# Attention and two mixtures on one core: the two layers of neighbouring blocks alternate, the gate's products follow the norm, and tasks that free a bank go first

## The chip, the cores and the metric

The kernel runs on one core of a Trainium2 chip. The metric is the device time of one execution in microseconds (us). Before the change it was 953.02 us, the median of three runs (952.83 to 954.03).

## The reference, cut to what matters

```
for each chunk c of 32 tokens:                 # attention, 4 x 8 heads, 768 tokens, head size 64
    k_full = mem_k (8 tokens) + k[16 left .. 8 right of the chunk]
    a   = softmax(q_c @ k_full.T / sqrt(64));  out = a @ v_full
x = out as (3072 tokens, 512)
h = x @ w_in                                   # first mixture: 512 -> 2048
g = where(h >= 1, h, where(h <= -1, 0, (h + 1)**2 / 4))
x = g @ w_out                                  # 2048 -> 512
xn = x / (norm(x) + 1e-6); logits = xn @ en.T / tau   # gate over 8 experts
e  = argmax(logits); gate = softmax(logits)[e]
out = gate * (relu(x @ w1[e]) @ w2[e])         # second mixture: 512 -> 1024 -> 512
```

All results are float32. The kernel splits a float32 operand into a high and a low float16 part and adds the products high*high, high*low and low*high.

## The kernel before, in words

**Blocks.** The 3072 tokens are cut into 8 blocks (`j`, 0 to 7) of 384 tokens. A block is 4 attention units (`u`) of 96 tokens, each of two halves (`a`, 4 heads each), and 3 tiles of 128 tokens for the second layer and the gate. The 2048 hidden features are 16 chunks (`fc`) of 128.

**Stages of a block.** First layer: for each chunk two steps of six matmuls (`l1_mm`, L441), into one PSUM bank of 128x384. Its evacuation is `l1_ev` (ScalarE), `l1_mx` (VectorE, L453, reads the bank last), `l1_mn` (VectorE, L457), `l1_hi` (ScalarE, L460) and `l1_lo` (VectorE, L463). Second layer: block 0 goes chunk by chunk, nine matmuls each over its three tiles at once (three banks); later blocks go tile by tile (`l2_mm`, L467 to L469). The second layer of block 0 also needs the weights `w_out`, which ScalarE and VectorE unpack from 64-bit floats (`conv_*`, L398 to L425), as they do `w_in` before.

**Gate of a block**, in this order: squares (`sq`, ScalarE), root on GpSimd (`grt`), norm on VectorE (`gno`, L504 to L519), transposes of the tiles by DMA (`xt`), the products with the experts on TensorE (`dot`, L495, 24 small matmuls into one bank), logits on VectorE (`glo`, L526 to L534, which read that bank), the first maximum (`gfi`, L542 to L547), weights (`gst`), ranks on TensorE (`grk`, L561 and L562, one more bank), and places on VectorE (`gpo`, L568 to L576, which read that bank).

**Banks.** PSUM is dealt in rings: `mm` with three banks (first layer, second layer, `dot`, `grk`), `PT` with two (attention's transposes, and two of five chunks of the first layer from block 2 on), `S` with two (scores), `X` with one. A ring is served in turn: the next task in `mm` takes the bank of the task three before it, and waits until what reads that one (its `frees`) is done.

**Attention** of a later block runs between the layers of a block. On VectorE a half costs `mx` (L290), `rc` (L312, L315) and four `ab` (L347); a unit costs copies and remainders of k, q and v (`k1` L248, `k` L253, `t1` L257, `t` L261, `vl` L266) and `xhl` (L385). On TensorE a half is a group of score matmuls (L281, or L283 and L284) and one of L367, or L369 to L371.

**Order.** `mixture` records all this as tasks with needs, engine and a cost from the table `COST`; `Plan.order` lists them twice backward and forward and writes one order for every engine. Among the tasks that could start at about the same time it takes the one that is wanted first. Every engine then works through its list in order, so a task that waits holds all that stand behind it on its engine. From the loop over the second mixture's later slots on, the order is written by hand.

Of the kernel before, what the change touches and what calls it, by code (L numbers as in the profile page):

```python
# [28 lines left out]
UB = 4  # L29
BT = UB * QU  # L30
NB = NT // BT
TB = BT // 128
NTILE = NT // 128
NFC = FF1 // 128
# [12 lines left out]
    cf=0.4, mk=1.5, k=2.2, K=4.0, c=2.3, v=1.1, pk=0.95, pt=0.73, pv=0.53, pk1=0.34, pkl=1.13, pt1=0.27, ptl=0.87, pvl=0.6,  # L47
    scc=1.72, scp=0.88, sc=0.47, mx=0.6, mb=0.1, sm=1.37, r1=0.1, rc=0.15, nm=0.6, trc=0.65, tr=0.34, ev=0.37, eh=1.0, el=0.8,
    td=1.25, avc=1.3, avp=0.68, av=0.52, xh=0.38, xl=0.47, ca=(0.58, 0.43), cv=0.34, cb=0.6, cs=0.6, cc=0.53, cd=0.6,
    l1=0.98, r4=0.47, mu=0.47, mn=0.47, hi=0.43, lo=0.47, l2=1.95, l2t=1.3, x2=0.49, sq=0.62, x2l=0.6, xt=1.25, dot=2.4,  # L50
    pad=0.4, emb=0.5, esq=0.6, ert=0.9, ein=1.9, etr=0.4, ehi=0.2, elo=0.2, grt=0.9, gno=1.6, glo=1.2, gfi=1.5, gst=0.8,
    grk=0.1, gpo=1.7, ga=2.6, w=2.3, wh=0.95, wl=1.13, xd=1.25, m1=2.62, mh=0.49, ml=0.6, m2=1.3, mo=0.57, ms=1.0, fbc=0.193,
    fbk=2.2, fbm=1.87, fbl=3.4, fbp=2.1, fbi=0.7, fbt=3.4, fac=0.175, fak=2.6, fal=1.4, fap=0.42, fai=0.5, fat=1.436)
# [1 line left out]
WIN = 0.019  # L55
PASSES = 3
CAE, ABUF = 'AD', 2
RINGS = dict(S=2, mm=3, PT=2)
PTJ = 2
BIG = 12582912.0  # L60

C_ID, C_I128, C_I39, C_I8, C_VT, C_TR = 0, 128, 256, 296, 304, 328
# [2 lines left out]


NUDGE = {}


class Plan:  # L70
# [14 lines left out]
    def run(self, pre, post, wanted, rings):  # L85
        free, held = defaultdict(float), defaultdict(list)
        missing = {t["n"]: len(t[pre]) for t in self.tasks}
        at = {}
        ready = [t for t in self.tasks if not missing[t["n"]]]
        done = []  # L90
        while ready:
            best = None
            for t in ready:
                if rings and t["ring"]:
                    h = held[t["ring"]]
                    k = len(h) - RINGS[t["ring"]]
                    extra = [self.named[x] for x in h[max(k, 0):max(k + len(t["frees"]), 0)] if x in self.named]
                    if any(x["n"] not in at for x in extra):
                        continue
                else:  # L100
                    extra = ()
                for w, c in list(zip(t["where"], t["cost"]))[:None if rings else 1]:
                    b = free[w]
                    for x in t[pre] + list(extra):
                        e, v = at[x["n"]]
                        d, u = (x, v) if rings else (t, w)
                        b = max(b, e + LAT[1 if u == "S" else 2 * (v == w)])
                    if best is None or (round(b / WIN), wanted[t["n"]], b + c) < best[0]:
                        best = ((round(b / WIN), wanted[t["n"]], b + c), t, b, c, w)
            _, t, b, c, w = best  # L110
            ready.remove(t)
            free[w] = b + c
            at[t["n"]] = (b + c, w)
            done.append((b, len(done), t, w))
            if rings and t["ring"]:
                held[t["ring"]] += t["frees"]
            for x in t[post]:
                missing[x["n"]] -= 1
                if not missing[x["n"]]:
                    ready.append(x)  # L120
        assert len(done) == len(self.tasks)
        return at, done
# [28 lines left out]
def moe_chain(ctx, tc, qd, kd, vd, win, wout, emb, tau, w1, w2, tmask, kmask, qp, kp, cf32, cf16, out):  # L151
# [275 lines left out]
    l1p = {}  # L427

    def l1_ring(j, fc):
        return "PT" if j >= PTJ and fc % 5 > 2 else "mm"  # L430

    def l1_mm(j, fc, part):
        xh, xl = xt[j]
# [224 lines left out]
    def mixture():  # L658
# [4 lines left out]
        def add(k, n, f, where, needs=(), cost=None, ring=None, frees=()):  # L663
            done[k, n] = pl.add((k, n), f, where, COST[cost or k], [x if isinstance(x, dict) else done.get(x) for x in needs], ring, frees)
# [107 lines left out]
        def weights(s, c, needs):  # L772
# [4 lines left out]
            add("wh", 8 * s + c, lambda w: split_w(s, c), "A", [("w", 8 * s + c), *needs])  # L777
            add("wl", 8 * s + c, lambda w: split_lo(s, c), "D", [("wh", 8 * s + c)])

        for u in range(UB):  # L780
            attention(u)
        for c in range(NRAW):
            load(c)
        for j in range(NB):
            i = start[j]
            if j == 0:
                for c in range(NFC):
                    conv(c)
            if j == NB - 1:
                n = (("fat", 0),)  # L790
            else:
                n = ()
            for fc in range(NFC):
                m = NFC * j + fc
                xs = [(x, u) for x in ("xh", "xl") for u in range(UB * j, UB * j + UB)]
                pe_slot(("l1", j, fc, 0), i, [("cc", fc), *xs, *n], "l1", ring=l1_ring(j, fc), frees=[("mu", m)])
                pe_slot(("l1", j, fc, 1), i + 1, [("cd", fc)], "l1")
                i += 2
                evac(j, m, fc)
                if j == NB - 1 and fc == 0:  # L800
                    for h in range(2):
                        add("ga", h, lambda w, h=h: gather(h), "G", [prev, ("ga", h - 1)])
                    for c in range(8):
                        add("w", c, lambda w, c=c: load_w(0, c), "S", [prev, ("w", c - 1)])
                if j == NB - 1 and fc % 2 == 1:
                    weights(0, fc // 2, [prev])
                    if fc == NFC - 1:
                        inputs(0, [prev])
            if j + 1 < NB:
                for u in range(UB * (j + 1), UB * (j + 2)):  # L810
                    attention(u)
            if j == 0:
                for c in range(NFC, 2 * NFC):
                    conv(c)
                for fc in range(NFC):
                    k = dict(ring="mm", frees=[("x2l", t) for t in range(TB)]) if fc == 0 else {}
                    pe_slot(("l2", 0, fc), i + fc, [("cd", NFC + fc), ("lo", fc), ("hi", fc)], "l2", **k)
                cds = [("cd", c) for c in range(2 * NFC)]
                add("pad", 0, lambda w: pads(), "G", cds)
                add("emb", 0, lambda w: emb_load(), "S", [("cf", 0)])  # L820
                add("esq", 0, lambda w: emb_sq(), "A", [("emb", 0)])
                add("ert", 0, lambda w: emb_root(), "G", [("esq", 0)])
                add("ein", 0, lambda w: emb_inv(), "D", [("ert", 0)])
                add("etr", 0, lambda w: emb_tr(), "P", [("ein", 0)], ring="mm", frees=[("elo", 0)])
                add("ehi", 0, lambda w: emb_hi(), "A", [("etr", 0)])
                add("elo", 0, lambda w: emb_lo(), "D", [("ehi", 0)])
            for t in range(TB):
                n = TB * j + t
                if j > 0:
                    for fc in range(0, NFC, 2):  # L830
                        m = NFC * j + fc
                        k = dict(ring="mm", frees=[("x2l", n)]) if fc == 0 else {}
                        pe_slot(("l2", j, t, fc), i, [("lo", m), ("lo", m + 1)], "l2t", **k)
                        i += 1
                last = ("l2", j, t, NFC - 2) if j else ("l2", 0, NFC - 1)
                add("x2", n, lambda w, n=n: l2_ev(n, p2[n % TB]), "A", [last, ("gst", j - 2), ("x2", n - 1), ("pad", 0)])
                add("sq", n, lambda w, n=n: g_sq(n, p2[n % TB]), "A", [("x2", n), ("sq", n - 1), ("glo", j - 2)])
                add("x2l", n, lambda w, n=n: l2_lo(n, p2[n % TB]), "D", [("x2", n), ("sq", n)])
                add("xt", n, lambda w, n=n: g_xt(n), "S", [("x2l", n), ("dot", j - 1), ("xt", n - 1)])
            add("dot", j, lambda w, j=j: g_dot(j), "P", [("xt", n), ("elo", 0)], ring="mm", frees=[("glo", j)])  # L840
            add("grt", j, lambda w, j=j: g_root(j), "G", [("sq", n)])
            add("gno", j, lambda w, j=j: g_norm(j), "D", [("grt", j), ("ein", 0)])
            add("glo", j, lambda w, j=j: g_logit(j), "D", [("gno", j), ("dot", j), ("gpo", j - 2), ("gst", j - 2)])
            add("gfi", j, lambda w, j=j: g_first(j), "D", [("glo", j), ("gfi", j - 1)])
            add("gst", j, lambda w, j=j: g_store(j), "D", [("gfi", j)])
            add("grk", j, lambda w, j=j: g_rank(j), "P", [("gfi", j), ("mk", 0)], ring="mm", frees=[("gpo", j)])
            add("gpo", j, lambda w, j=j: g_pos(j), "D", [("grk", j), ("gpo", j - 1)])
            if (j + 1) * TB == TA:
                add("fac", 0, lambda w: fa_count(), "P", [("gfi", j)], ring="S", frees=[("fak", 0)])
                add("fak", 0, lambda w: fa_key(), "D", [("fac", 0)])  # L850
                add("fal", 0, lambda w: fa_look(), "D", [("fak", 0), ("gpo", j)])
                add("fap", 0, lambda w: fa_place(), "D", [("fal", 0)])
                add("fai", 0, lambda w: fa_ids(), "P", [("fap", 0)], ring="S", frees=[("fat", 0)])
                add("fat", 0, lambda w: fa_table(), "D", [("fai", 0)])
# [492 lines left out]
```

## Time and profile before

| | |
|---|---|
| time, median of three runs | 953.02 us (952.83 to 954.03) |
| the profiled execution's own time | 952.98 us |
| its span, first to last instruction | 951.1 us |
| TensorE matmuls busy | 874.3 us (92%) |
| VectorE busy | 697.5 us (73%) |
| ScalarE busy | 557.5 us (59%) |
| mean granted TensorE clock | 0.983 |

The span is the time that the instructions take; the execution's own time is 1.9 us more. A clock of 1.00 is 2.4 GHz and 0.50 is 1.2 GHz. The busy shares are means over stages that differ, so stages are looked at one by one.

### The profile page before, as it was taken

To read this page: it belongs to the slowest core of one execution; us is meant where nothing else is said; L and a number is where in the kernel's file an instruction comes from. 1 tells how busy PE (TensorE), PEld (TensorE's weight loads), DVE (VectorE), ACT (ScalarE), POOL (GpSimd) and SP (SyncE) were. 2 spreads that over 40 slices of the span, in tenths; PEclk is the share of its full clock that TensorE was granted. 3 is DMA by queue.
4 is the path that set the end of the run, shared out by engine and by line. 5 is a ranking of instruction groups with operands and counts; after the bars stand their busy time and mean duration, and the time that the engine had idled before them with its cause. 6 is when DMAs were issued, how large, how long until landed. Compare 5 with 4: busy or idle time off the path is not lost.

```text
span 951.1 us, 17049 instructions
## 1 busy us (share of the span) xinstructions
PE 874.3 (92%) x6072; PEld 525.5 (55%) x6072; DVE 697.5 (73%) x1601; ACT 557.5 (59%) x1397; POOL 71.7 (8%) x70
## 2 busy tenths in 40 slices
PE   2899999997588999989999999999999899999995
PEld 2666555444354555555555454554666567766663
DVE  6999999988997896897895294494764745556650
ACT  4767869777857846846855142363434655555551
POOL 0000000000000000000000100200021222222221
PEclk9999999999799999999999999999999999999998
DMA  9964536357534723632411200466222223322550
GB/s 267 263 196 124 194 101 161 101 156 191 141 123 109 153 73 65 185 85 44 70 45 28 40 34 12 138 196 162 72 68 78 68 68 85 84 67 68 138 163 25
DMA packets 118700, 105.64 MB, mean 111 GB/s; under 512 B 92286, under 2 KB 92548, under 8 KB 118608
## 3 DMA queue, kind: packets, MB, share of 16 engines
q1 hardware_dynamic: 114608, 91.80, 36.7%
q0 software_dynamic: 4000, 12.69, 4.1%
q8 instruction: 49, 0.80, 0.4%
q14 instruction: 43, 0.35, 0.1%
HBM read 112.09 MB, written 12.94 MB: 131 GB/s over the span
## 4 chain that ended last, share of the span: by engine, by line
issue 77%; DVE 10%; DMA 6%; POOL 3%; PE 1%; ACT 1%; POOLq 0%; SPq 0%; DVEq 0%; ACTq 0%
DMA out<-o,fbid 5%; DVE cvt L409 2%; POOL xg L1118 2%; DVE cvt L413 1%; DMA out<-o,faid 1%; DVE wo L425 1%; DVE cvv L405 1%; DVE t L453 1%; DVE mx L290 1%; DVE r L457 1%; POOL nsa L499 1%; DVE wi L425 1%; DVE g L463 1%; PE S L281 1%; POOL out L1185 1%
## 5 line engine op out<-in xcount | busy, mean ns | idle before, releaser
L441 PEld LDWEIGHTS <-wi 128*128 128x128 f16 x1536 | 149.9, 99 | 110.5 <-issue 19.0
L441 PE MATMUL mm<-xhl,wi 128*128 128x384 f16 x1104 | 197.4, 335 | 8.2 <-DVE t L453 5.6
L467 PE MATMUL mm<-wo,g 128*128 128x512 f16 x384 | 146.4, 381 | 0.5 <-DVE t L453 0.5
L469 PE MATMUL mm<-wo,g 128*128 128x512 f16 x384 | 146.0, 380 | 0.0
L468 PE MATMUL mm<-wo,g 128*128 128x512 f16 x384 | 146.0, 380 | 0.0
L460 ACT ACTIVATE g<-r 128x384 f16<-128x384 f32 x128 | 66.9, 523 | 78.5 <-DVE r L457 78.4
L1158 DVE SCALAR_TENSOR_TENSOR g<-PT,g 128x512 f16<-128x512 f32 (+1 forms) x52 | 34.8, 670 | 93.0 <-ACT g L1153 93.0
L441 PE MATMUL PT<-xhl,wi 128*128 128x384 f16 x432 | 74.3, 326 | 0.0
L1110 DVE SCALAR_TENSOR_TENSOR wi<-stg,wi 128x1024 f16<-128x1024 f32 x56 | 66.1, 1219 | 8.2 <-ACT wi L1105 8.2
L463 DVE TENSOR_TENSOR g<-r,g 128x384 f16<-128x384 f32 x128 | 70.3, 549 | 1.9 <-ACT g L460 1.2
L457 DVE SCALAR_TENSOR_TENSOR r<-r,t 128x384 f32<-128x384 f32 x128 | 70.5, 551 | 0.7
L1153 ACT ACTIVATE g<-PT 128x512 f16<-128x512 f32 (+1 forms) x52 | 30.2, 581 | 68.5 <-PE PT L1147 68.5
L447 ACT ACTIVATE r<-mm,two 128x384 f32<-128x384 f32 x92 | 53.0, 577 | 26.4 <-PE mm L441 24.8
L342 ACT ACTIVATE ab<-e,rc 96x128 f16<-96x128 f32 x184 | 58.7, 395 | 13.1 <-issue 3.8
L306 ACT ACTIVATE e<-S,mx 96x128 f32<-96x128 f32 x184 | 64.1, 363 | 0.8 <-DVE ab L347 0.7
L469 PEld LDWEIGHTS <-g 128*128 128x128 f16 x384 | 37.6, 98 | 45.7 <-issue 0.6
L1110 DVE SCALAR_TENSOR_TENSOR wo<-stg,wo 128x1024 f16<-128x1024 f32 x48 | 56.4, 1219 | 8.4 <-ACT wo L1105 7.9
L467 PEld LDWEIGHTS <-g 128*128 128x128 f16 x384 | 37.5, 98 | 38.6 <-issue 0.3
L468 PEld LDWEIGHTS <-g 128*128 128x128 f16 x384 | 37.6, 98 | 36.3 <-issue 1.0
L1105 ACT ACTIVATE wi<-stg 128x1024 f16<-128x1024 f32 x56 | 57.0, 1046 | 0.0
L476 DVE SCALAR_TENSOR_TENSOR x2a<-mm,x2a 128x512 f16<-128x512 f32 x24 | 16.5, 687 | 55.0 <-ACT junk L484 54.9
L1182 ACT ACTIVATE o<-mm,xg 128x512 f32<-128x512 f32 x25 | 17.2, 687 | 66.2 <-issue 41.0
(263 smaller groups left out, 1786.2 us busy)
## 6 DMA issues: line engine op xcount, KB each, us to landing
stg<-w SPq DMA_DIRECT2D x104, 512.0 KB
kraw<-kd SPq DMA_DIRECT2D x23, 512.0 KB
qraw<-qd SPq DMA_DIRECT2D x23, 384.0 KB
vraw<-vd SPq DMA_DIRECT2D x30, 256.0 KB
x2d<-x2a SPq DMA_DIRECT2D x8, 780.0 KB
x2a<-win SPq DMA_DIRECT2D x8, 512.0 KB
x2a<-wout SPq DMA_DIRECT2D x7, 512.0 KB
kraw<-kp SPq DMA_DIRECT2D x7, 256.0 KB
```

The source lines that it names most:

```text
L306: act.activation(e[:QU, i, :], w["s"][:QU, i, :], AF.Exp, bias=nb[:QU, i:i + 1], scale=0.125 if plain(a // 2) else 1.0, accum_out=sm[:QU, ...
L342: act.activation(w["ab"][:QU, 0, i, :], w["e"][:QU, i, :], AF.Copy, scale=w["rc"][:QU, i:i + 1])
L441: pe.matmul(l1p[fc], w[fc][:, k, :], x[:, k, :], start=(part == 0 and n == 0), stop=(part == 1 and n == 5))
L447: act.activation(g32[fc], l1p[fc], AF.Relu, bias=two[:, 0:1], scale=2.0 ** -13)
L457: dve.scalar_tensor_tensor(out=r4, in0=r4, scalar=4.0, in1=t4s.pop(fc), op0=ALU.min, op1=ALU.mult)
L460: act.activation(gh[fc], g32[fc], AF.Copy)
L463: dve.tensor_tensor(gl[fc], g32.pop(fc), gh[fc], ALU.subtract)
L467: pe.matmul(p, gh[fc][:, ts], woh[fc], start=(fc == 0), stop=False)
L468: pe.matmul(p, gh[fc][:, ts], wol[fc], start=False, stop=False)
L469: pe.matmul(p, gl[fc][:, ts], woh[fc], start=False, stop=(fc == NFC - 1))
L1105: act.activation(hi, stg[c], AF.Copy, scale=64.0 if c < NK else 512.0)
L1110: dve.scalar_tensor_tensor(out=lo, in0=stg[c], scalar=sc, in1=hi, op0=ALU.mult, op1=ALU.subtract)
```

## The change

Four edits. (1) The first layer of block 1 is no longer behind the second layer of block 0 but between its chunks: after chunk `fc` of the second layer (from `fc` = 3 on) comes chunk `fc - 3` of block 1's first layer. Its banks come from the ring `PT` alone, since the second layer of block 0 holds all three banks of `mm`. The attention of block 2 is recorded after both. (2) `dot` needs `gno`, and its entry in the cost table is smaller. (3) Where the forward pass picks among tasks that could start together, `glo`, `gpo`, `x2l` and `elo`, which all free a bank of `mm`, come before all others. (4) The counting of steps (`start`) follows. No arithmetic is added or removed.

```diff
-    l1=0.98, r4=0.47, mu=0.47, mn=0.47, hi=0.43, lo=0.47, l2=1.95, l2t=1.3, x2=0.49, sq=0.62, x2l=0.6, xt=1.25, dot=2.4,
+    l1=0.98, r4=0.47, mu=0.47, mn=0.47, hi=0.43, lo=0.47, l2=1.95, l2t=1.3, x2=0.49, sq=0.62, x2l=0.6, xt=1.25, dot=0.65,
+AHEAD = 3
+RUSH = ("glo", "gpo", "x2l", "elo")
...
-                    if best is None or (round(b / WIN), wanted[t["n"]], b + c) < best[0]:
-                        best = ((round(b / WIN), wanted[t["n"]], b + c), t, b, c, w)
+                    r = (round(b / WIN), wanted[t["n"]] - 1e4 * (rings and t["key"][0] in RUSH), b + c)
+                    if best is None or r < best[0]:
+                        best = (r, t, b, c, w)
...
     def l1_ring(j, fc):
-        return "PT" if j >= PTJ and fc % 5 > 2 else "mm"
+        return "PT" if j == 1 or j >= PTJ and fc % 5 > 2 else "mm"
...
+        def first(j, fc, n=()):
+            i, m = start[j] + 2 * fc, NFC * j + fc
+            xs = [(x, u) for x in ("xh", "xl") for u in range(UB * j, UB * j + UB)]
+            pe_slot(("l1", j, fc, 0), i, [("cc", fc), *xs, *n], "l1", ring=l1_ring(j, fc), frees=[("mu", m)])
+            pe_slot(("l1", j, fc, 1), i + 1, [("cd", fc)], "l1")
+            evac(j, m, fc)
...
-            for fc in range(NFC):
-                m = NFC * j + fc
...
+            for fc in range(NFC if j != 1 else 0):
+                first(j, fc, n)
...
-            if j + 1 < NB:
+            if j + 1 < NB and j != 1:
                 for u in range(UB * (j + 1), UB * (j + 2)):
                     attention(u)
...
                     pe_slot(("l2", 0, fc), i + fc, [("cd", NFC + fc), ("lo", fc), ("hi", fc)], "l2", **k)
+
+                    if fc >= AHEAD:
+                        first(1, fc - AHEAD)
+                for fc in range(NFC - AHEAD, NFC):
+                    first(1, fc)
+                for u in range(2 * UB, 3 * UB):
+                    attention(u)
...
-            add("dot", j, lambda w, j=j: g_dot(j), "P", [("xt", n), ("elo", 0)], ring="mm", frees=[("glo", j)])
             add("grt", j, lambda w, j=j: g_root(j), "G", [("sq", n)])
             add("gno", j, lambda w, j=j: g_norm(j), "D", [("grt", j), ("ein", 0)])
+            add("dot", j, lambda w, j=j: g_dot(j), "P", [("xt", n), ("elo", 0), ("gno", j)], ring="mm", frees=[("glo", j)])
```

What this makes of the engines' lists is seen at three places. The line numbers of the changed kernel are 3 higher there. First TensorE at the second layer of block 0: `wo_94` and `wo_95` are the high and low weights of the second layer, `wi_86` low weights of the first, `PT<-cf,e` a transpose of attention. Before, between its chunks 3 and 4:

```order
L467 LDWEIGHTS g
L467 MATMUL mm<-wo_94,g 128x512
L468 LDWEIGHTS g
L468 MATMUL mm<-wo_95,g 128x512
L469 LDWEIGHTS g
L469 MATMUL mm<-wo_94,g 128x512
L325 MATMUL PT<-cf,e 128x96 x4
L467 LDWEIGHTS g
```

and now the end of block 1's first chunk, which stands between the same two chunks:

```order
L444 LDWEIGHTS wi_86
L444 MATMUL PT<-xhl,wi_86 128x384
L470 LDWEIGHTS g
L470 MATMUL mm<-wo_94,g 128x512
L471 LDWEIGHTS g
L471 MATMUL mm<-wo_95,g 128x512
L472 LDWEIGHTS g
L472 MATMUL mm<-wo_94,g 128x512
```

The twelve matmuls of a first-layer chunk moved in between; attention's transposes that stood there are ahead of it or behind. Second VectorE in the first layer of block 2, where the gates of blocks 0 and 1 stand. Before, the logits of block 1 (`lg`) and the places of block 0 (`rk`) came behind attention (`ab`, `mx`, `k`, `vl`):

```order
L290 TENSOR_REDUCE mx<-S 96x4
L253 SCALAR_TENSOR_TENSOR k_3095<-kraw,k_3095 64x1024
L347 SCALAR_TENSOR_TENSOR ab<-e,rc,ab 96x128 x4
L266 SCALAR_TENSOR_TENSOR vl<-vraw,vh 128x512
L526 COPY lg<-mm 128x24
L527 TENSOR_TENSOR lg<-lg,mm 128x24
L528 TENSOR_TENSOR lg<-lg,nrm 128x24
L530 TENSOR_REDUCE mxl<-lg 128x3
L533 TENSOR_TENSOR eq<-lg,mxl 128x24
L534 TENSOR_TENSOR lg<-lg,mxl 128x24
L568 TENSOR_TENSOR rk<-mm,oh 128x24
```

and now the places of block 0 come behind the first evacuation (`t`, `r`) of block 2's first layer:

```order
L479 SCALAR_TENSOR_TENSOR x2a<-mm,x2a 128x512
L456 SCALAR_TENSOR_TENSOR t_2766<-mm,r_2748 128x384
L293 TENSOR_REDUCE mx<-S 96x4
L460 SCALAR_TENSOR_TENSOR r_2748<-r_2748,t_2766 128x384
L350 SCALAR_TENSOR_TENSOR ab<-e,rc,ab 96x128 x4
L571 TENSOR_TENSOR rk<-mm,oh 128x24
L573 TENSOR_REDUCE pos<-rk 128x3
```

They moved from behind the evacuation of the fifth chunk to behind that of the first. The `dot` of block 1 and its logits left this layer: they now stand in the second layer of block 2. Third TensorE in the first layer of block 6, at the ranks of block 5 (`oh`, `rs`; `wi_80` and `wi_88` are the weights of chunks 4 and 5). Before they stood ahead of chunk 5, whose banks are of `mm` again:

```order
L441 LDWEIGHTS wi_88
L441 MATMUL PT<-xhl,wi_88 128x384
L561 LDWEIGHTS ch
L561 MATMUL mm<-oh,ch 128x24
L562 LDWEIGHTS ch
L562 MATMUL mm<-rs,ch 128x24
L441 LDWEIGHTS wi_80
L441 MATMUL mm<-xhl,wi_80 128x384
```

and now between the two steps of chunk 5:

```order
L444 LDWEIGHTS wi_80
L444 MATMUL mm<-xhl,wi_80 128x384
L564 LDWEIGHTS ch
L564 MATMUL mm<-oh,ch 128x24
L565 LDWEIGHTS ch
L565 MATMUL mm<-rs,ch 128x24
L444 LDWEIGHTS wi_80
L444 MATMUL mm<-xhl,wi_80 128x384
```

They moved back by one step of six matmuls, and past the point where chunk 5 takes its bank: so chunk 7 now takes the bank that chunk 5 held, and chunk 10 that of the ranks.

## Rows read from the trace of the kernel before

**Rows 1.** Part 1 of the page: busy us, share of the span, instructions.

```profile
PE 874.3 (92%) x6072; PEld 525.5 (55%) x6072; DVE 697.5 (73%) x1601; ACT 557.5 (59%) x1397; POOL 71.7 (8%) x70
```

**Rows 2.** Windows between first evacuations: engines' busy us (count), granted clock, DMA share, GB/s.

```profile
0.00:60.97 60.97, 38.12 (x203) 30.20 (x204) 49.54 (x114) 36.98 (x122) 0.32 (x6) 1.00 0.85 249
60.97:143.45 82.48, 79.41 (x533) 47.56 (x531) 82.33 (x179) 63.09 (x175) 2.80 (x3) 1.00 0.48 147
143.45:181.92 38.47, 35.34 (x276) 20.93 (x274) 38.33 (x97) 35.17 (x102) 0.00 (x0) 1.00 0.48 119
181.92:227.40 45.48, 40.76 (x319) 21.70 (x319) 40.05 (x113) 31.69 (x107) 1.29 (x1) 0.96 0.69 184
227.40:286.07 58.67, 43.59 (x341) 26.89 (x340) 56.31 (x160) 42.56 (x132) 0.00 (x0) 0.88 0.46 132
286.07:328.09 42.02, 39.77 (x307) 20.67 (x307) 32.09 (x80) 33.78 (x120) 0.79 (x1) 0.96 0.59 142
328.09:362.37 34.28, 31.55 (x204) 18.50 (x202) 30.61 (x85) 17.18 (x36) 0.06 (x1) 0.95 0.25 59
362.37:403.94 41.57, 41.35 (x322) 21.52 (x321) 32.06 (x79) 33.72 (x120) 0.78 (x1) 1.00 0.58 143
```

**Rows 3.** Timeline of TensorE: start, us, line, tiles, count, idle before and its releaser.

```profile
222.56 0.24 PE L369 MATMUL X<-at,vh 128*64 128x96 f16 x2 [3.52 <-DMA at<-ab]
...
233.62 0.75 PE L495 MATMUL mm<-ent,x2x 128*128 128x16 f16 x24
...
252.12 0.30 PE L369 MATMUL X<-at,vh 128*64 128x96 f16 x2 [4.22 <-DMA at<-ab]
```

**Rows 4.** Timeline of VectorE around 252 us.

```profile
252.75 0.17 DVE L526 COPY lg<-mm 128x24 f32<-128x24 f32 x1
...
253.91 0.17 DVE L568 TENSOR_TENSOR rk<-mm,oh 128x24 f32<-128x24 f32 x1
```

**Rows 5.** Windows of 5 us in the same stretch, columns as in group 2.

```profile
245.00:250.00 5.00, 1.71 (x20) 1.58 (x20) 4.97 (x16) 5.00 (x21) 0.00 (x0) 0.50 0.43 165
250.00:255.00 5.00, 2.88 (x25) 2.10 (x25) 4.62 (x18) 2.83 (x10) 0.00 (x0) 0.50 0.74 221
```

**Rows 6.** Groups of VectorE: busy us, mean ns of one, idle before.

```profile
L347 DVE SCALAR_TENSOR_TENSOR ab<-e,rc,ab 96x128 f16<-96x128 f32 x184 | 52.5, 342 | 3.3 <-ACT ab L342 3.2
...
L290 DVE TENSOR_REDUCE mx<-S 96x4 f32<-96x512 f32 x60 | 40.7, 678 | 15.8 <-PE S L281 9.0 <-PE S L284 6.7
...
L253 DVE SCALAR_TENSOR_TENSOR k<-kraw,k 64x1024 f16<-64x1024 f32 x23 | 28.1, 1223 | 0.7
...
L261 DVE TENSOR_TENSOR t<-qraw,t 64x768 f16<-64x768 f32 x23 | 21.7, 944 | 0.1
...
L266 DVE SCALAR_TENSOR_TENSOR vl<-vraw,vh 128x512 f16<-128x512 f32 x23 | 15.7, 681 | 0.8 <-ACT vh L243 0.7
```

**Rows 7.** Timeline of TensorE: a group of scores and the first layer behind it.

```profile
142.40 0.22 PE L283 MATMUL S<-k,t 67*96 67x128 f16 x1
...
142.87 1.14 PE L441 MATMUL mm<-xhl,wi 128*128 128x384 f16 x6
```

**Rows 8.** Timeline of TensorE: waits at the gates of later blocks.

```profile
342.27 3.77 PE L441 MATMUL mm<-xhl,wi 128*128 128x384 f16 x12 [1.95 <-DVE t L453]
...
418.12 2.11 PE L441 MATMUL mm<-xhl,wi 128*128 128x384 f16 x12 [1.95 <-DVE t L453]
...
553.05 0.17 PE L561 MATMUL mm<-oh,ch 128*128 128x24 f16 x1 [1.23 <-DVE oh L545]
...
620.52 0.17 PE L561 MATMUL mm<-oh,ch 128*128 128x24 f16 x1 [0.96 <-DVE oh L545]
...
623.28 2.11 PE L441 MATMUL mm<-xhl,wi 128*128 128x384 f16 x12 [0.22 <-DVE rk L568]
```

**Rows 9.** Timelines around the gate of block 5: the norm's end on VectorE, the products on TensorE.

```profile
546.43 0.23 DVE L519 TENSOR_SCALAR nrm<-nrm,rtau 128x3 f32<-128x3 f32 x1
...
547.17 0.74 PE L495 MATMUL mm<-ent,x2x 128*128 128x16 f16 x24 [0.20 <-DVE t L453]
```

More of the change, by code (lines that the diff above doesn't have):

```diff
@@ L784, in mixture @@
         for j in range(NB):
-            i = start[j]
+            i = start[j] + 2 * NFC
             if j == 0:
@@ L792, in mixture @@
                 n = ()
-            for fc in range(NFC):
-                m = NFC * j + fc
[L795 to L799, printed above, removed]
+            for fc in range(NFC if j != 1 else 0):
+                first(j, fc, n)
                 if j == NB - 1 and fc == 0:
```

## The prediction, made before the changed kernel had run

> **What bounds the kernel now.** I read the busy times first, then windows cut where VectorE first evacuates a block, then the waits of TensorE in the worst window. TensorE's matmuls are busy 92% of the span [rows 1], so only some 77 us of idle time can be won, and whatever runs at 1.2 GHz. No single engine explains the windows [rows 2]. They are cut at the first evacuations (L453) of block 0 (60.97), block 1 (143.45), the last chunk of block 1 (181.92), block 2 (227.40), its last chunk (286.07), block 3 (328.09), its last chunk (362.37) and block 4 (403.94). From 60.97 to 181.92 VectorE is busy 120.7 of 121.0 us: it is the bound, and TensorE merely follows. From 328.09 on TensorE is busy 72.9 of 75.9 us and VectorE has a sixth to spare. Between them lies the loss: from 227.40 to 286.07 TensorE is idle 15.1 of 58.7 us, and VectorE is busy 56.3.
>
> What VectorE does there matters more than that it is busy. The products of block 1's gate were issued at 233.62 [rows 3]; the logits that read their bank, and the places of block 0 that read the bank before it, run only at 252.75 and 253.91 [rows 4], behind attention of later blocks. Two of the three `mm` banks are shut for some 19 us, chunk 5 of the layer cannot take one, and the written order fills TensorE's queue with attention that waits in its turn (3.52 and 4.22 us in front of two groups [rows 3]). TensorE does 1.71 and 2.88 us of work in two windows of 5 us, at a granted clock of 0.50 [rows 5].
>
> **The change, part by part.** Its instructions are those of before, so all is a matter of what stands where. I price it at the first evacuation of block 3 (328.09 now), then go on from there.
>
> *Work in front of that mark.* Up to it VectorE is busy 298.7 us (the sum of the first six windows [rows 2]), so it idles 29.4. Counting the changed list of VectorE up to the same evacuation, it holds less attention: three `mx` and three pairs of `rc`, two halves' `ab` (eight instructions), one unit's copies and remainders (`k`, `t` and their copies), two `vl`. With the means [rows 6] that is 3 x 0.68 + 8 x 0.34 + 1.22 + 0.94 + 2 x 0.68 = 8.3 us, and some 1.7 for the small ones: about 10, of which I take 9, since such instructions overlap by a tenth in the timeline. That work is done later.
>
> *Idle time in front of that mark.* Of the 29.4 us, 11.4 come before the first evacuation, with inputs arriving, and 0.3 in the two windows after it [rows 2]; both stay. The rest, 5.4 + 2.4 + 9.9 = 17.7 us, is VectorE waiting for a TensorE that was itself held up, or had no attention left to give it, since that had been done in the stall. With the places of block 0 behind the first evacuation of block 2, and block 1's products out of that layer, the stall has no cause. In the changed list the layer of block 2 holds three halves of attention, two units' preparation and one whole gate less than before, 18 us, and the second layer behind it 16 more: VectorE gets as much to do as TensorE in both. Between 0.15 us of idle time in a window (the two full ones) and 17.7 (nothing mended) I take 5, nearer to the full windows because VectorE's work is what fills the list there. The mark comes 9 + 12.7 = 21.7 us earlier. The bounds: all 17.7 won is 26.7, none is 9.
>
> *The alternation itself* I cost at nothing and credit with nothing beyond this: both the second layer of block 0 and the first of block 1 lie in windows where VectorE is full [rows 2], and the conversions, evacuations and attention that fill it are only dealt out differently. Its cover is that VectorE sets the pace. What it risks is the ring: block 1 had three banks and now has two, shared with transposes, so TensorE may wait for an evacuation behind a conversion. A rule of the skill speaks against it. From 60.97 to 181.92 TensorE waits in places too, 6.2 us in all, and the granted clock is 1.00 throughout [rows 2]; by these rows small waits cost their own length only. The Trainium skill (TensorE: Matmul & The Clock Gate, "A second HAM failure mode: psum-queue depth-cycling") describes a kernel that goes round PSUM banks each iteration, where TensorE idles a little between groups and the clock swings between its two levels; by it the sum would be the slower rival's below. The trace agrees with it only for the starved windows, at 0.50.
>
> *Products after the norm.* `dot` now waits for `gno`. Behind it on TensorE stand steps of the next first layer, and VectorE would lack their evacuations. At block 5's gate the norm ends at 546.66 and the products start at 547.17 already [rows 9]: there the wait is nothing. It would be a cost where VectorE is backed up, in block 2; there the products were moved into the second layer, whose matmuls have banks of their own. I take 0, bounds 0 and 2 us.
>
> *Blocks 3 and 4.* Now chunk 7 waits 1.95 us in each, for the bank that chunk 5 held [rows 8], and after the first the twelve matmuls take 3.77 us in place of 2.11, at half the clock: 5.6 us. In the changed lists the ranks stand behind chunk 7 in both blocks, so it takes another bank. The postponed attention comes in here: three score groups of 0.47 us [rows 7] and one of L369 to L371 of the same order, 1.9 us on TensorE; VectorE, with 13.2 us idle in the two windows of block 3 [rows 2], takes its 9. With 1 us for new waits: -5.6 + 1.9 + 1 = -2.7.
>
> *Blocks 5 to 7.* In these the ranks now stand inside chunk 5, and chunk 7 takes chunk 5's bank, as it did in blocks 3, 4 and 7. That order costs 1.95, 1.95 and (0.96 + 0.22 + 0.22) us there [rows 8]; about 1.6 in each of three blocks is 4.8. What it replaces is 1.23 and a few tenths in block 6, 1.4 in block 7 and next to nothing in block 5, 3 together. I take +2, bounds 0 and +6 (a fall of the clock as in block 3 behind two of them).
>
> *The sum.* -21.7 - 2.7 + 2 = -22.4 us. Against the profiled execution: span 951.1 - 22.4 = 928.7, and 1.9 around it gives 930.6; that execution took 952.98, the median is 953.02. **I predict 931 us.** With the bounds, 26.7 + 4 gives 922 at the low end, and 9 + 2.7 - 6 gives 947 at the high end.
>
> **The rivals.**
>
> *More than that.* All idle time after the first evacuation goes, the first layer starts some us earlier (scores of two halves of block 1 now stand behind its first step), and no gate waits: 26.7 + 3.5 + 3.7 = 34 us, 919. For it: VectorE idles 0.3 us in 121 when its list is full. Against it: TensorE would have to follow a saturated VectorE without a slip for 270 us.
>
> *Two banks are too few.* In the alternation TensorE waits 0.5 to 1 us more for each of block 1's 16 chunks, and VectorE then waits for TensorE. That takes 8 to 16 us off: 939 to 947. For it: TensorE idles 6.2 us there even with three banks [rows 2]. Against it: VectorE sets the pace, and a pair of chunks needs no more of TensorE than of VectorE.
>
> *The gain is given back.* The postponed attention is late where block 3 and 4 need its result, and TensorE waits there for what it does not wait for in block 2. Then the time is that of before but for the small gates, 949 to 955. Against it: 13 us of idle VectorE in block 3 alone for 9 us of work.
>
> *Slower: the clock falls in the alternation.* If the two banks make TensorE idle between all groups as in the starved windows, it runs at 1.2 GHz through the stretch. Its work there is 114.8 us in the windows from 60.97 to 181.92, about half of it in the alternation; at half the clock that is up to 57 us more, 931 + 57 = 988. It decides when the clock is down for more than some 22 us of matmul work, which uses up the gain. Against it: the clock stayed at 1.00 in that stretch with TensorE idle 5% of the time, and fell only behind single waits of 1.95 us and more, or in the starved windows [rows 5, 8]. By the rule of the skill named above it would have fallen; that hangs on rows that do not show it.
>
> **How the numbers follow.** The sum: 0.66, with 923 to 938 as its own range. More: 0.10. Two banks too few: 0.14. Given back: 0.05. Slower: 0.05. Less than 0.2% (1.9 us) cannot be told from no change here. Faster by more than that is the sum, the two cases beside it and a fifth of the given back: 0.91; the same, 0.03; slower, 0.06 with the rest of the given back. The range that leaves out two in ten cuts off the lower part of the 919 case, the upper part of the two-bank case and the last two: 922 to 942.
>
> **What would show it.** Right: between the first evacuations of blocks 2 and 3 the new trace has VectorE nearly full and some 88 us in place of 100.7; `lg` and `rk` run within a few us of `dot` and of the ranks; the clock stays at 1.00 from 227 to 300; chunk 7 of blocks 3 and 4 does not wait, that of blocks 5 to 7 does, for 1 to 2 us. Wrong: waits of L444 for VectorE in the alternation, a clock of 0.50 there, or waits for attention in the layers of blocks 3 and 4. The most doubtful step is the 5 us of idle time that I leave VectorE; it alone moves the result by -5 to +13.

## The result and the profile after

The changed kernel took 931.72 us, median of four runs (929.89 to 933.45), against 953.52 us (952.83 to 955.90) beside it: a ratio of 0.9767, 95% interval 0.9740 to 0.9794. Its profiled execution was the slowest of the four, 933.45 us with a span of 931.7.

Part 1 of its page answers to [rows 1]: TensorE is busy 6.7 us less with the same 6072 matmuls, as less of its work runs at 1.2 GHz (mean clock 0.993 in place of 0.983), and VectorE 4.3 less.

```profile
PE 867.6 (93%) x6072; PEld 522.0 (56%) x6072; DVE 693.2 (74%) x1600; ACT 557.2 (60%) x1398; POOL 73.7 (8%) x70
```

Windows of the changed kernel, cut as in [rows 2] but with blocks 0 and 1, now one stretch, in one row (57.37 to 176.00); the columns are those of [rows 2].

```profile
0.00:57.37 57.37, 36.15 (x200) 29.21 (x201) 46.06 (x107) 35.31 (x112) 0.32 (x6) 1.00 0.95 240
57.37:176.00 118.63, 115.17 (x775) 68.80 (x774) 117.46 (x266) 91.63 (x262) 4.99 (x3) 0.99 0.49 142
176.00:219.33 43.33, 40.77 (x338) 21.16 (x337) 40.95 (x121) 35.56 (x118) 0.91 (x1) 1.00 0.72 190
219.33:258.43 39.10, 36.18 (x288) 21.91 (x287) 38.73 (x100) 35.06 (x108) 0.00 (x0) 1.00 0.41 92
258.43:305.43 47.00, 41.97 (x356) 22.39 (x354) 45.15 (x130) 36.70 (x126) 0.85 (x1) 1.00 0.79 196
305.43:340.06 34.63, 33.65 (x242) 20.22 (x236) 33.68 (x101) 26.14 (x70) 0.00 (x0) 1.00 0.30 72
340.06:380.73 40.67, 38.09 (x301) 20.00 (x301) 34.86 (x83) 31.73 (x113) 0.85 (x1) 1.00 0.77 187
```

The layer of block 2 (219.33 to 258.43) takes 39.1 us in place of 58.7, with TensorE idle 2.9 us in place of 15.1 and the clock at 1.00 in place of 0.88. The first evacuation of block 3 comes at 305.43, 22.7 us earlier; that of block 5 comes 24.6 us earlier (452.57 against 477.15), and the end 19.4.

The two places that the stall hung on answer to [rows 3, 4]. Timeline of TensorE, the ranks of block 0 and the products of block 1:

```profile
219.46 0.17 PE L564 MATMUL mm<-oh,ch 128*128 128x24 f16 x1 [0.23 <-DVE x2a L479]
...
272.97 0.75 PE L498 MATMUL mm<-ent,x2x 128*128 128x16 f16 x24
```

and timeline of VectorE, the places that read the first, the end of the norm, and the logits that read the second:

```profile
221.91 0.17 DVE L571 TENSOR_TENSOR rk<-mm,oh 128x24 f32<-128x24 f32 x1
...
269.79 0.23 DVE L522 TENSOR_SCALAR nrm<-nrm,rtau 128x3 f32<-128x3 f32 x1
...
275.30 0.17 DVE L529 COPY lg<-mm 128x24 f32<-128x24 f32 x1
```

The banks are read 2.4 and 2.3 us after they were begun, in place of 25.9 and 19.1. What is lost again shows in block 6, on TensorE's timeline: a wait of 4.13 us for two VectorE instructions of the count of tokens (the matmuls of the "ids" below), and 3.4 us at 0.50 behind it.

```profile
538.86 0.61 PE L940 MATMUL S<-fasv,rhot 128*128 128x4 f16 x18 [4.13 <-DVE fasv L934]
539.33 3.77 PE L444 MATMUL PT<-xhl,wi 128*128 128x384 f16 x12
```

In the kernel before, the same matmuls wait 0.46 us.

### The profile page after: what moved, and what is told of

Read it like the earlier page. It is cut to its first block, busy times and chain, and to the rows that moved or that the text cites. A ratio compares the mean times of both kernels' runs of the same rounds, so it can differ in the third digit from the quotient of the medians.

```text
span 931.7 us, 17019 instructions
## 1 busy us (share of the span) xinstructions
PE 867.6 (93%) x6072; PEld 522.0 (56%) x6072; DVE 693.2 (74%) x1600; ACT 557.2 (60%) x1398; POOL 73.7 (8%) x70
## 5 line engine op out<-in xcount | busy, mean ns | idle before, releaser
L444 PE MATMUL mm<-xhl,wi 128*128 128x384 f16 x912 | 160.7, 328 | 1.2 <-ACT xhl L383 0.6
L444 PE MATMUL PT<-xhl,wi 128*128 128x384 f16 x624 | 111.3, 331 | 0.0
L345 ACT ACTIVATE ab<-e,rc 96x128 f16<-96x128 f32 x184 | 58.7, 398 | 16.7 <-issue 11.2
L450 ACT ACTIVATE r<-mm,two 128x384 f32<-128x384 f32 x76 | 43.8, 577 | 19.5 <-PE mm L444 16.1
```

Source lines behind the costliest of these rows:

```text
L345: act.activation(w["ab"][:QU, 0, i, :], w["e"][:QU, i, :], AF.Copy, scale=w["rc"][:QU, i:i + 1])
L444: pe.matmul(l1p[fc], w[fc][:, k, :], x[:, k, :], start=(part == 0 and n == 0), stop=(part == 1 and n == 5))
L450: act.activation(g32[fc], l1p[fc], AF.Relu, bias=two[:, 0:1], scale=2.0 ** -13)
```

## The experiments

The theory at the outset ("shut banks"): the gain comes from the readers of the gate's banks (logits, places) running at once, so that the order no longer holds the layer's chunks back. Its rival: the alternation of the two layers makes it. All kernels compute the same; the diffs are against the changed kernel. The stretch to look at is the layer of block 2, from its first evacuation to its last. One row of windows is shown for each kernel, with the columns of [rows 2]; its length less TensorE's busy time is TensorE's idle time. All times at the end are medians.

**1. The alternation alone.**

```diff
-RUSH = ("glo", "gpo", "x2l", "elo")
+RUSH = ()
...
-            add("dot", j, ..., [("xt", n), ("elo", 0), ("gno", j)], ...)
+            add("dot", j, ..., [("xt", n), ("elo", 0)], ...)
```

(with `dot=2.4` as before). 

> The alternation alone, with the old place of the products and no task put first. Theory 'shut banks' (the gain is the end of the stall in block 2, where two mm banks wait for the logits of block 1 and the places of block 0): in this order these stand behind attention again, so the stall of some 15 us on TensorE between the first evacuations of block 2 and block 3 stays, and only the earlier start is won: -2 to -7 us, near 949. Rival 'alternation' (mixing the two layers is what evens out VectorE's work): at least two thirds of the gain, -14 us or more, 939 or less.

Measured: 947.82 us, ratio 0.9956 (0.9941 to 0.9971), as "shut banks" had it. The stall is longer than in the kernel before: TensorE idles 18.6 us in the layer, at a clock of 0.76.

```profile
216.21:281.27 65.06, 46.44 (x355) 29.23 (x354) 63.30 (x168) 48.33 (x150) 0.00 (x0) 0.76 0.51 144
```

**2. The gate's two edits without the alternation.**

```diff
-        return "PT" if j == 1 or j >= PTJ and fc % 5 > 2 else "mm"
+        return "PT" if j >= PTJ and fc % 5 > 2 else "mm"
...
-                    if fc >= AHEAD:
-                        first(1, fc - AHEAD)
```

(and block 1's layer recorded like the others). 

> Products after the norm and bank-freeing tasks first, with the layers of blocks 0 and 1 in the old order and ring. 'Shut banks': the stall in block 2 is gone, -15 to -20 us, near 936, idle time of TensorE between the first evacuations of blocks 2 and 3 under 7 us. 'Alternation': -7 us or less, 946 or more.

Measured: 936.04 us, 0.9829 (0.9800 to 0.9858), as "shut banks" had it.

```profile
222.01:261.97 39.96, 37.63 (x300) 22.92 (x298) 39.80 (x104) 37.01 (x117) 0.00 (x0) 1.00 0.43 109
```

The stall is gone without any alternation. The first evacuation of block 3 is 24.4 us earlier; 3.8 us of that go by block 4's, behind a wait of 3.78 us for VectorE in front of a group of attention at 343.30, and 3.4 us at 0.50.

**3. The products behind the norm alone** (no alternation, `RUSH = ()`). 

> Only the products after the norm, with their smaller entry in the cost table. 'Shut banks', read from this order: the logits of block 1 stand right behind its products and the places of block 0 behind its ranks, so the stall goes although nothing is put first: -11 to -17 us, near 939. If putting tasks first is what matters: -5 us or less.

Measured: 943.08 us, 0.9911 (0.9879 to 0.9942): 1.4 us short of what was expected. The window is mended, with places 8.2 and logits 3.2 us behind what they read:

```profile
227.20:265.46 38.26, 36.44 (x313) 22.73 (x312) 37.92 (x103) 35.59 (x111) 0.00 (x0) 0.98 0.34 81
```

but of 20.0 us at block 3's first evacuation 8.4 are given back by block 4's, at waits of 1.63 and 4.18 us and 6.8 us at 0.50.

**4. The preference alone** (no alternation, `dot` without `gno`). 

> Only the bank-freeing tasks put first. In this order the products of block 1 are issued long before its norm, which is not put first, so their bank is shut until the norm has run and the logits cannot go: 'shut banks' has one bank shut for some 15 us, one short stall, -4 to -10 us, near 946. If putting them first is what matters: -14 us or more.

Measured: 948.82 us, 0.9958 (0.9939 to 0.9977): 3.9 us less than before, at the edge of the 4 to 10 expected. Timeline of TensorE, then of VectorE:

```profile
239.14 0.32 PE L498 MATMUL mm<-ent,x2x 128*128 128x16 f16 x7
```

```profile
257.12 0.23 DVE L522 TENSOR_SCALAR nrm<-nrm,rtau 128x3 f32<-128x3 f32 x1
...
258.31 0.17 DVE L529 COPY lg<-mm 128x24 f32<-128x24 f32 x1
```

The products are issued 18.2 us before the norm ends, which nothing prefers; the logits follow it at once. One bank is held for 19.2 us, and TensorE idles 9.5 us in the layer.

**5. Alternation and products behind the norm** (`RUSH = ()`). 

> The change without the preference for tasks that free a bank (alternation, and the gate's products behind the norm). Theory 'shut banks': the preference is worth about 7 us behind the products' new place (952.7 - 9.6 for the products alone against 952.7 - 16.7 with both), and the alternation 4 to 5 more whatever stands beside it: 936 to 941 us, with a wait left over in block 3 behind which the clock is at 0.50. Rival 'the alternation makes the gain': 930 to 933, as in the whole change.

Measured: 950.41 us, 0.9969 (0.9945 to 0.9994). Both theories missed it. The norm ends at 219.4, the products come at 223.81, the logits only at 245.28; then the ranks of block 1 at 249.44, their places at 270.26.

```profile
221.54:283.49 61.95, 46.62 (x358) 28.74 (x357) 59.86 (x161) 47.70 (x146) 0.00 (x0) 0.83 0.49 131
```

**6. Alternation and preference, `dot` without `gno`.** 

> The change without the gate's products behind the norm (alternation, and the preference). Theory 'shut banks': the bank of block 1's products stays shut from their issue to a norm that nothing prefers, so the stall in block 2's first layer stays: 941 to 947 us, first evacuation of block 3 only 8 to 16 us earlier than before the change, and a clock of 0.50 for more than 10 us in front of it. Rival 'the alternation makes the gain': 930 to 936 and no such stretch.

Measured: 928.62 us, 0.9738 (0.9688 to 0.9788), 3.1 us less than the whole change by the medians; the intervals of the two ratios overlap (0.9740 to 0.9794 for the whole change). My expectation of a stall was wrong: the norm ends at 221.2 and the products stand at 224.90 behind it without being told to, the logits come at 228.79.

```profile
221.14:260.88 39.74, 35.93 (x318) 22.05 (x316) 39.42 (x104) 36.61 (x114) 0.00 (x0) 1.00 0.34 84
```

The rival's time came nearer, but not by its reason: runs 1 and 5 have the alternation as well, and stall. So what counts is not which edit is there but when the readers run. Runs 8 to 10 put that to the test.

**7. The ids later.** `order` adds what stands in `NUDGE` to a task's time when it sorts the order; those that need the task or its bank move behind it.

```diff
-NUDGE = {}
+NUDGE = {("fai", 0): 6.0}
```

> The whole change, with the two matmuls of the ids (L940) three chunks later on TensorE in block 6, and nothing else. In the changed kernel TensorE waits 4.13 us there for L934 and then runs 3.4 us at 0.50. Theory 'a wait of its own, behind a late operand': both go, 4 to 6 us less than the whole change, 925.5 to 928 us, the clock at 1.00 through blocks 5 to 7. Rival 'the wait only shows a VectorE that is behind': TensorE waits for VectorE a little later, within 1.5 us of the whole change.

Measured: 923.91 us (923.66 to 924.72), 0.9688 (0.9638 to 0.9737), 7.8 us less than the whole change where 4 to 6 were expected. The order of every engine is that of the whole change up to these matmuls. They come at 538.48 and wait for nothing; the clock stays at 1.00 through all eight blocks. From block 6's first evacuation to block 7's it takes 62.54 us in place of 68.53: 6.0 us. The spans differ by 9.8: another 1.9 us lie before block 1 ends (see the last section), and 1.8 behind block 7.

**8. Places of block 0 late**, nothing else meant:

```diff
-NUDGE = {}
+NUDGE = {("gpo", 0): 20.0}
```

> The whole change, with the places of block 0 (five small VectorE instructions that read the bank of its ranks) put some 20 us further back on VectorE, behind evacuations and attention; TensorE's list is written around the bank that stays shut, as before the change. Theory 'shut banks': one bank held that long brings the stall back in part, the first evacuation of block 3 comes 5 to 14 us later than in the whole change, 937 to 946 us, with a stretch at 0.50 in block 2's first layer. Rival 'the place of five small instructions is nothing, the order of the rest makes the gain': within 2 us of the whole change.

Measured: 934.70 us, 0.9793 (0.9743 to 0.9844): 3.0 us more than the whole change, between the two expectations. TensorE's timeline:

```profile
232.67 0.24 PE L372 MATMUL X<-at,vh 128*64 128x96 f16 x2 [1.71 <-DMA at<-ab]
...
235.64 0.30 PE L372 MATMUL X<-at,vh 128*64 128x96 f16 x2 [2.52 <-DMA at<-ab]
...
236.27 4.01 PE L444 MATMUL mm<-xhl,wi 128*128 128x384 f16 x16
```

and VectorE's:

```profile
238.15 0.17 DVE L571 TENSOR_TENSOR rk<-mm,oh 128x24 f32<-128x24 f32 x1
```

This shows how a shut bank costs: no matmul of the layer waits for it. Chunk 6 starts 1.9 us before the places read, so it does not have their bank (the text ahead of the prediction lets a task always take the bank of the task three before it; that rule sets its place in the order); it was held back by the order, in which it stands behind the places, while two groups of attention that stand ahead of it are not ready. In the kernel before it is the same: from 227 to 262 all waits of TensorE but 0.2 us stand in front of attention, and chunk 5 follows a group of scores at 253.62 without a pause, before the places of block 0 read (253.91 [rows 4]), so it is not their bank that it took. Here the loss is 3.3 us in the layer (42.41 long), for one bank of three. In run 4 one bank held as long goes with a layer 11 us longer than in run 2 (50.71 against 39.96); the order there has let 10 us more of VectorE's work into it (49.63 us against 39.29). Why it lets so much more ahead in the one and not in the other stays open.

**9 and 10. Half of the preference each.**

```diff
-RUSH = ("glo", "gpo", "x2l", "elo")
+RUSH = ("glo", "gpo")
```

> The whole change, but only the two readers of the gate's banks (logits and places) are preferred, the second layer's remainders and those of the experts' rows are not. Theory 'shut banks of the gate': within 4 us of the whole change, 928 to 936 us, and places and logits of blocks 0 and 1 within 5 us of what they read. Rival 'preferring the second layer's remainders, which come 24 times, is what pays': 943 to 952.

```diff
-RUSH = ("glo", "gpo", "x2l", "elo")
+RUSH = ("x2l", "elo")
```

> The whole change, but only the second layer's remainders and those of the experts' rows are preferred, logits and places are not. Theory 'shut banks of the gate': places of block 0 and of block 1 are some 20 us behind their ranks again, the first layer of block 2 stalls, 944 to 954 us with over 10 us at 0.50 in it. Rival (remainders): 928 to 936.

Measured: 931.43 us with the gate's readers preferred, 0.9772 (0.9749 to 0.9796), and 951.75 us with the remainders preferred, 0.9991 (0.9973 to 1.0009). The first row of windows is run 9's, the second run 10's; the third fence is VectorE's timeline in run 10, with the places of block 0 (ranks at 218.8) and of block 1 (ranks at 249.3).

```profile
217.95:256.85 38.90, 35.52 (x287) 21.56 (x286) 38.57 (x98) 34.06 (x101) 0.08 (x1) 1.00 0.41 94
```

```profile
215.46:283.04 67.58, 45.91 (x379) 28.66 (x377) 65.57 (x180) 50.50 (x161) 0.29 (x1) 0.85 0.52 142
```

```profile
242.03 0.18 DVE L571 TENSOR_TENSOR rk<-mm,oh 128x24 f32<-128x24 f32 x1
...
272.02 0.18 DVE L571 TENSOR_TENSOR rk<-mm,oh 128x24 f32<-128x24 f32 x1
```

With alternation and products behind the norm in both, the preference for 16 small tasks (logits and places of eight blocks) decides over 20 us; the preference for the 24 remainders of the second layer and those of the experts is worth nothing that can be measured. More than the place of those 16 differs, though: the preference sorts the order anew, VectorE's lists part at its 49th instruction (31 us), and in the layer of block 2 run 10 has 27.0 us more of VectorE's work (65.57 against 38.57). That the late readers alone make the 20 us is thus not shown. Run 8, which keeps most of the order, made one of them late and lost 3.0 us; both late at once, in an order otherwise the same, was not run.

**11. Four more waits moved.**

```diff
-NUDGE = {}
+NUDGE = {("fai", 0): 6.0, ("sc", 34): 2.1, ("av", 34): 2.1, ("sc", 43): 2.1, ("av", 42): 2.1}
```

> The whole change with the ids later as in the run before that moved them, and four groups of attention for which TensorE waits (1.1, 1.1, 1.5 and 1.9 us) each one or two steps later on it. Theory 'each is a place that is too early, and VectorE keeps up': 3 to 5 us less than with the ids alone, 919 to 921.5 us. Rival 'VectorE is behind there, the wait moves on with the group': 922.5 to 925.

Measured: 931.86 us, 0.9782 (0.9759 to 0.9805), 8 us more than with the ids alone; both theories missed it. The four waits are nearly gone (0.61 us is left of 5.6), but at block 3's last evacuation nothing is won (339.95, against 338.15 in run 7, a difference that is there already before block 2), and then a group of attention waits, with the clock down behind it:

```profile
349.00 0.30 PE L372 MATMUL X<-at,vh 128*64 128x96 f16 x2 [3.64 <-DMA at<-ab]
```

VectorE is not behind there: it is busy 1.62 of the 5 us from 347.5. Nor are this group's scores and remainders late: they run 1.8 us behind run 7, as everything does there (scores at 301.48 against 299.68, the last remainder done at 326.29 against 324.48). What is late is the DMA that transposes for it. Timeline of SyncE's queue, first run 7, then run 11:

```profile
340.66 1.22 SPq L356 DMA_TRANSPOSE at<-ab  x1
```

```profile
343.22 0.33 SPq L228 DMA_DIRECT2D kraw<-kd  x1
343.60 0.43 SPq L229 DMA_DIRECT2D qraw<-qd  x1
344.14 2.81 SPq L356 DMA_TRANSPOSE at<-ab  x2
```

By the tasks' needs the transpose comes behind the group of half 42, one of the four moved, and in the new order it fell behind the loads of a later unit, which in run 7 stand behind it. It is issued 3.5 us later than in run 7, 1.7 more than the common 1.8. At block 4's first evacuation the kernel is 5.1 us behind run 7, 1.8 of which were there before; the end is 6.0 us behind by the spans. The rest of the 8 us lies between executions: this profiled one was the fastest of its four, 2.1 us below the median, that of run 7 0.2 below its own.

**12. One wait moved in the kernel of run 6.**

```diff
-NUDGE = {}
+NUDGE = {("sc", 47): 5.0}
```

> Alternation and preference without the products behind the norm (928.6 us), with one group of scores (half 47, for which TensorE waits 3.16 us there and then runs 6.8 us at 0.50) two and a half chunks later on TensorE. Theory 'a place that is too early': 4 to 6.5 us less, 922 to 924.5 us, and the clock at 1.00 through block 3. Rival 'the wait moves on': 927 to 930.

Measured: 929.10 us, 0.9753 (0.9728 to 0.9778); the rival was right. The scores of half 47 no longer wait (3.16 us in run 6), but the group of half 42, which did not wait, does:

```profile
339.87 0.30 PE L372 MATMUL X<-at,vh 128*64 128x96 f16 x2 [2.89 <-DVE xhl L388]
```

**All of them side by side**, in order of time. Idle time and clock are TensorE's in the layer of block 2; the delays are from the ranks of block 0 to their places, and from the products of block 1 to their logits.

| kernel | us | idle, clock | delays, us |
|---|---|---|---|
| 7 ids later | 923.91 | 2.9, 1.00 | 2.4, 1.7 |
| 6 alternation, preference | 928.62 | 3.8, 1.00 | 1.8, 3.9 |
| 12 as 6, one wait later | 929.10 | 3.8, 1.00 | 1.8, 3.9 |
| 9 preference for the gate only | 931.43 | 3.4, 1.00 | 2.4, 1.7 |
| whole change | 931.72 | 2.9, 1.00 | 2.4, 2.3 |
| 11 four waits later | 931.86 | 2.9, 1.00 | 2.4, 2.4 |
| 8 places late | 934.70 | 5.1, 0.96 | 19.0, 2.3 |
| 2 both gate edits | 936.04 | 2.3, 1.00 | 0.2, 2.9 |
| 3 products behind the norm | 943.08 | 1.8, 0.98 | 8.2, 3.2 |
| 1 alternation | 947.82 | 18.6, 0.76 | 38.9, 30.6 |
| 4 preference | 948.82 | 9.5, 0.90 | 0.2, 19.2 |
| 5 alternation, products | 950.41 | 15.3, 0.83 | 0.3, 21.5 |
| 10 preference for remainders | 951.75 | 21.7, 0.85 | 23.2, 2.8 |
| before | about 953 | 15.1, 0.88 | 25.9, 19.1 |

In runs 5 and 10 the places of block 1 are late too, by 20.8 and 22.8 us. VectorE is busy 96% or more of the window in every one of them but run 8 (93%): in a stall it does not idle, it does attention that is wanted later, while TensorE, which is the busier engine from block 3 on, idles. I take that TensorE time to be what does not come back; no run isolates it.

Where the layer stops supports the theory. In four of these kernels there are chunks of the layer of block 2 that start over 10 us behind the chunk before, seven in all, and in no other kernel is there one. Each starts between 2.8 us before and 0.9 us after a late reader of the gate's banks:

| kernel | chunk before starts | chunk starts | late reader |
|---|---|---|---|
| before | 236.12 | 253.62 | logits of block 1, 252.75 |
| 1 | 226.95 | 246.23 | logits of block 1, 249.01 |
| 1 | 246.23 | 259.62 | places of block 0, 260.42 |
| 5 | 231.70 | 245.60 | logits of block 1, 245.28 |
| 5 | 256.81 | 268.45 | places of block 1, 270.26 |
| 10 | 225.67 | 239.77 | places of block 0, 242.03 |
| 10 | 255.22 | 269.94 | places of block 1, 272.02 |

So the order holds the chunk until about its reader, and five of the seven start before that reader does. But a late reader does not always stop the layer: before the change the places of block 1 come 19.3 us behind their ranks (258.32, 277.66), and no gap follows. What makes the difference stays open.

## Why the prediction was right, and where it was not

**The mark at block 3.** Right in size and in both halves. Up to it VectorE's work is 288.4 us (sum of the first five windows after) against 298.7: 10.3 us postponed, 9 predicted. Its idle time is 17.1 against 29.4: 12.3 us won, 12.7 predicted. The mark moved 22.7 us, 21.7 predicted. That the preference for the readers of the gate's banks ends the stall is shown by runs 9 and 10. The way in which late readers cost was told too simply: chunk 5 was held back by the order (run 8 and the table of gaps), not by a bank for which TensorE waited, and one bank held for 19 us cost 3 us in run 8; how the whole 20 come about is shown in part only. One detail of the argument was more than was needed: block 1's products need not leave the layer of block 2 (run 6 has them in it), their logits have to follow them.

**The alternation at nothing.** At the mark this was right. Run 2, which lacks the alternation, has its first evacuation of block 0 3.2 us later (60.58 against 57.37), but with 3.5 us more of VectorE's work behind it (49.53 against 46.06). At block 3's first evacuation both have done the same work (288.1 and 288.4 us), and run 2 is 1.7 us ahead (303.72 against 305.43). Behind the mark it was mis-sized: at block 4's first evacuation run 2 is 2.7 us behind (383.40 against 380.73), after its wait of 3.78 us, and by the medians the whole change is 4.3 us faster. Alone the alternation is worth some 4 to 5 us (run 1). The two banks of the ring cost nothing that can be seen: TensorE idles 3.5 us from 57.37 to 176.00, against 6.2 in the stretch before, and there is one stretch of 3.4 us at 0.50. So the rival of two banks too few and the slower one did not come. The kernel that the Trainium skill (TensorE: Matmul & The Clock Gate, "A second HAM failure mode: psum-queue depth-cycling") describes has a clock that swings while it goes round its banks; this stretch, with a mean of 0.99, does not.

**Products after the norm.** No wait came of it (norm ended at 270.02, products at 272.97), as predicted. But without the edit and its entry in the cost table the kernel is 3.1 us faster by the medians (run 6). Its trace has no wait of the ids, which the whole change pays with 4.13 us and 3.4 us at 0.50; with the ids moved (run 7) the kernel that has the edit is 4.7 us faster than run 6. So it is not shown that the edit itself costs anything.

**Blocks 3 and 4.** Chunk 7's waits of 1.95 us are gone, as said. From block 3's first evacuation to block 5's it takes 147.14 us against 149.06: -1.9, where -2.7 was the sum. A wait of 1.90 us for late attention at 342.06 took the place of a part.

**Blocks 5 to 7.** The size was near by luck, the step failed: chunk 7 waits nowhere there. It does not take chunk 5's bank, as the prediction and the text ahead of it say: it starts at 464.11, 530.67 and 600.03, 2.1 to 4.1 us before VectorE has read chunk 5 out (466.23, 534.77, 603.62). The sum had a slip as well: the three waits that it averages make 1.8 us each, not 1.6. From block 5's first evacuation to block 7's last it takes 171.60 us against 168.71, +2.9 where I had +2, and the ids' wait and the half clock behind it are more than the whole of it: in run 7, without them, the stretch takes 165.58 us, 3.1 less than before the change. I had read the bank of chunk 5 and not what else the new order puts early.

**After block 7** the profiled execution loses 2.2 us more in the second mixture, whose order is the same. Run 6 wins 0.4 us there and run 7 loses 0.4, so I put it down to that execution, which was 1.7 us above the median. That the median came within 1 us of the forecast is in part luck: in the profiled execution the sum of -22.4 us came out as -19.4.

## What to carry to other kernels

When a bank or buffer is shared in an order that is fixed beforehand, put the few small instructions that read it last right behind what they read: here the preference for 16 tasks of six or seven instructions each decided 20 us of 950, and forcing a producer to be later (products behind the norm) did so only when nothing else delayed the reader. Look for the cost in front of other work, for the order holds back what would need the bank, and the waits stand elsewhere. And moving a work that waits further back pays where nothing close behind needs its result: the ids gave 7.8 us; groups in a chain of attention gave nothing or lost the 8 us again, since a transfer that needs the moved group fell back with it, or the next group waited in its place.

## What was not expected of the hardware

The same waits at the same place of the same order lower TensorE's clock in one execution and not in another. In the whole change and in run 7 the scores of the alternation wait 0.50 and 0.51 us, and then 1.73 us each (timeline of TensorE, first the whole change, then run 7):

```profile
144.86 0.22 PE L286 MATMUL S<-k,t 67*96 67x128 f16 x1 [0.50 <-ACT e L309]
146.81 0.22 PE L287 MATMUL S<-k,t 128*96 128x128 f16 x1 [1.73 <-DVE k L256]
```

```profile
143.66 0.22 PE L286 MATMUL S<-k,t 67*96 67x128 f16 x1 [0.51 <-ACT e L309]
145.60 0.22 PE L287 MATMUL S<-k,t 128*96 128x128 f16 x1 [1.73 <-DVE k L256]
```

Behind them the granted clock is 0.51 and 1.00, in windows from 147.0 to 150.5 of each (run 7 has 1.00 from 145.8 to 149.3 as well):

```profile
147.00:150.50 3.50, 3.50 (x19) 2.24 (x17) 3.49 (x11) 1.43 (x4) 0.00 (x0) 0.51 0.76 244
```

```profile
147.00:150.50 3.50, 3.05 (x23) 1.85 (x23) 3.50 (x10) 2.70 (x12) 0.00 (x0) 1.00 0.69 242
```

The order is the same up to there, and run 7 comes to it 1.2 us earlier. From the first evacuation of block 1 to its last it takes 63.54 us in the one and 62.82 in the other. Six more kernels have the same order up to 187 us: runs 8, 9 and 11 fall there too and take 63.5 to 63.6 us, runs 1, 6 and 12 do not and take 62.8. So such a fall costs about 0.7 us where VectorE sets the pace. A difference of that size between two profiles is thus no sign of an edit.
